# Turning x for the scores: TensorE transposes, or 32x32 squares and VectorE

## The chip, the cores and the metric

The kernel runs on one core of one Trainium2 chip. The metric is the time of one execution on the device in microseconds; lower is better. Runs are given as a median with the lowest and highest.

## What is computed

```python
def _attn_ref(x, state) -> np.ndarray:
    B, H, S, D = x.shape                     # 8, 8, 512, 64; state has Ns = 32 rows
    scale = 1.0 / np.sqrt(D)
    scores = scale * np.matmul(x, state.transpose(0, 1, 3, 2))
    ...
    xread = np.matmul(a, state)              # a: softmax of scores over the state rows
    scores2 = scale * np.matmul(state, x.transpose(0, 1, 3, 2))
    ...
    sread = np.matmul(a2, x)                 # a2: softmax of scores2 over the 512 tokens
    return np.concatenate([xread, sread], axis=2).astype(np.float32)

def _moe_ref(x, w_in, w_out) -> np.ndarray:  # 4352 tokens x 512, d_ff 2048
    h = x @ w_in
    g = h * (1.0 / (1.0 + np.exp(-1.702 * h)))
    return (g @ w_out).astype(np.float32)
```

Each batch of x meets its state in both directions, and the two results, side by side for all heads, go through an MLP. All of it is float32. `scores2` contracts over D, so TensorE needs x with D on the partitions (x turned); `sread` contracts over tokens and needs x as it lies in memory.

## The kernel before

The work goes batch by batch, b = 0 to 7. While the second matrix of the MLP is applied to batch b, the attention and the first matrix are prepared for batch b + 1. Batches 0 and 1 and the weights, which arrive as float64 words and are rounded on the chip, take the first part of the span, up to about 155 us. From b = 2 on the iterations are alike.

Products are made by Strassen's scheme of seven products, and inside some of these again (`strassen_low`). The seven outer products for a batch are called P1 to P7, and are run in the order P1, P2, P5, P6, P3, P7, P4. P1, P2 have two halves, "a" and "b". P5, P6, P3, P7 and P4 are, from b = 2 on, each seven small products of eight matmuls; after the i-th of these comes the slot "P5.i" and so on. Each small product ends in a PSUM bank, and VectorE adds it to an earlier one (L656), or ScalarE copies it (L660, L666). Three banks are used in turn, x, y and z: y takes products 2, 5 and 7, z takes 4 and 6, and a later product accumulates on what the earlier one left, so it waits until the add before it has read the bank.

The order of instructions on every engine is the order in which the program issues them; nothing is reordered. Waits between engines follow from the tiles that are read and written. `hooks_next(b)` is a table of the work for the next batch: the name of a slot, and the step that is issued there. `strassen_two` runs through the products and calls `hook(name)` at each slot. So the table decides what stands behind what in each engine's queue.

The steps that matter here, for batch b, in slots of the iteration b - 1:

- `load_x(b)`: four transfers of 256 KB, 128 tokens each, into the tile `xn` (one buffer, 16 KB a partition). They are issued from SyncE (SP) after the last product of the iteration b - 2. In between, the same buffer holds `low4`, the sums that P4 of the running iteration needs, which are loaded after `att_sread`.
- `att_xT(b, j)`: four TensorE transposes of 128x128 (L282) of two heads, and one copy to SBUF by ScalarE (L283). It is called for j = 0 to 3, in the slots P1a and P1b.
- `att_scores(b)`: 8 matmuls of 512 columns (L303), from the turned x, in P2a. Both softmaxes start from their result.
- `att_blocks`, `x_max`, `x_sub`, `x_exp`, `x_sum`, `x_inverse`, `x_scale`, `x_back`: the softmax over the state rows, after VectorE has turned the scores in squares of 32x32 (L334). At the end it turns them back (L429). g = 0, 1 are its two halves.
- `att_s_max`, `att_s_exp`, `att_s_norm`: the softmax over tokens.
- `att_sread(b)`: 64 matmuls with x as it lies (L462).
- `up_strassen(b)`: the first matrix of the MLP at the beginning of the iteration b; its products end in adds on VectorE (L1053). The last two of these follow the first half of P1.
- `s12`, `s3` (L523, L524, L529) and the L709 adds: sums of activations for the outer and inner products. `own6` places two of these steps into P6.
- `load_weights`: the 16 pieces of each weight matrix, issued from SP as room for them comes free (L168).

In memory, x is [batch, head, token, d], with rows of 64 floats. In the turned tile, 128 partitions are two heads (g) by 64 values of d, and the free side is j (four pairs of heads) by 512 tokens.

All transfers of the kernel are issued from SP. The framework gives each of them one of eight semaphores in turn, and a transfer waits for the one eight before it to land.

Of the kernel before, what the change touches and what calls it, by code (L numbers as in the profile page):

```python
# [10 lines left out]
FP32 = mybir.dt.float32  # L11
I32 = mybir.dt.int32
U32 = mybir.dt.uint32
AF = mybir.ActivationFunctionType
# [6 lines left out]
def kernel(  # L21
# [30 lines left out]
    nc = tc.nc  # L52

    B, H, S, D = x.shape
    Ns = state.shape[2]
    DM = H * D
    DF = moe_w_in.shape[1]
    P = 128
    NPR = P // Ns
    NG = H // NPR  # L60
    NF = DF // P
# [5 lines left out]
    HF, HN = NF // 2, DM // 2  # L67
    scale = float(1.0 / np.sqrt(D))
# [3 lines left out]
    out_x = out.rearrange("(b t) n -> b t n", b=B)[:, :S].rearrange("b (c q) n -> b c q n", c=SCH)  # L72
    out_s = out.rearrange("(b t) n -> b t n", b=B)[:, S:]
    x_v = x.rearrange("b h (c q) d -> b c q h d", c=SCH)
    st_v = state.rearrange("b (j g) n d -> b g j n d", g=NG)

    konst = ctx.enter_context(tc.tile_pool(name="konst", bufs=1))
    xpool = ctx.enter_context(tc.tile_pool(name="xpool", bufs=1))
# [44 lines left out]
            nc.tensor.matmul(ps, zeros[:, :P], zeros, start=True, stop=True)  # L123


    xn, stn = {}, {}

    def load_state(b):
        stn[b] = apool.tile([P, NG, D], FP32, tag="stn", name=f"stn_{b}", bufs=2)
# [3 lines left out]
    def load_x(b):  # L133
        if b == 1:
            xn[b] = sums[:, 0].rearrange("p (c h d) -> p c h d", c=SCH, h=H)
        else:
            xn[b] = xpool.tile([P, SCH, H, D], FP32, tag="xn", name=f"xn_{b}")
        for c in range(SCH):
            nc.sync.dma_start(xn[b][:, c], x_v[b, c])

    def x_heads(b, c, j):
        return xn[b][:, c, NG * j : NG * (j + 1)].rearrange("q g d -> q (g d)")
# [33 lines left out]
    for i, v in enumerate((8.0 * most, 8.0 * (most - least))):  # L176
        t = konst.tile([P, 1], FP32, name=f"edge_{i}")
# [90 lines left out]
    A = {b: {} for b in range(B)}  # L268
# [134 lines left out]
        t = a["e1"][:, g]  # L403
        nc.vector.tensor_tensor(out=t, in0=t, in1=a["mx"][:, g].to_broadcast((P, NB, Ns)), op=ALU.subtract)

    def x_exp(b):
        nc.scalar.activation(out=A[b]["e1"], in_=A[b]["e1"], func=AF.Exp, scale=scale)

    def x_sum(b, g):
        a = A[b]  # L410
# [102 lines left out]
    def quarters(key, u, ntok):  # L513

        g, half = G[key, u], ntok // 2
        return g[:, :, :half], g[:, :, half:ntok]

    def s12(key, u, ntok):

        half = ntok // 2  # L520
        (a11, a21), (_, a22) = quarters(key, u, ntok), quarters(key, HF // 2 + u, ntok)
        s1, s2 = S1[:, 2 * u : 2 * u + 2, :half], S2[:, 2 * u : 2 * u + 2, :half]
        nc.vector.tensor_tensor(out=s1, in0=a21, in1=a22, op=ALU.add)  # L523
        nc.vector.tensor_tensor(out=s2, in0=s1, in1=a11, op=ALU.subtract)  # L524
# [156 lines left out]
    def strassen_two(key, dst, hooks, a4):  # L681
# [4 lines left out]
        g = [G[key, u] for u in range(HF)]  # L686
# [30 lines left out]
        def low_banks():  # L717
            return [bank_o[1], *(psH.tile([P, FC], FP32, tag="h", name=f"low_{key}") for _ in range(2))]
# [50 lines left out]
        o, h0, h1 = low_banks()  # L769
# [6 lines left out]
        else:  # L776
# [9 lines left out]
            o, h0, h1 = low_banks()  # L786
# [33 lines left out]
        def y_of(u0, o):  # L820
            return lambda u, i: g[u0 + u][:, :, o + P * i : o + P * (i + 1)]
# [3 lines left out]
        own6 = {}  # L825
        if not plain:
            steps12, left12 = sums(y_of(NU, 0), r)
            own6 = {5: steps12[:1], 6: steps12[1:2]}
        lowly("P6", left_of(S2, q1, q2, q4), T2, low_a, banks, k2, own6)
        if not plain:  # L830
            low_load(3, 0)
# [2 lines left out]
        if plain:  # L834
# [5 lines left out]
            o, h0, h1 = low_banks()  # L840
            lowly("P7", left3, T3, low_b, [h0, h1, o], k3, {})
        else:
            hook("P6")
            p3 = o01
            o, h0, h1 = low_banks()
# [7 lines left out]
            o, h0, h1 = low_banks()  # L853
# [11 lines left out]
        if not plain:  # L865
            o, h0, h1 = low_banks()
# [15 lines left out]
    def hooks_next(b):  # L882

        h = {}

        def at(name, fn, *args):
            h.setdefault(name, []).append((fn, args))

        at("P1a", att_state, b)
        at("P1a", att_xT, b, 0)  # L890
        at("P1b", att_xT, b, 1)
        at("P1b", att_xT, b, 2)
        at("P1b", att_xT, b, 3, True)
        at("P2a", att_scores, b)
        at("P2a", att_M, b, 0)
        at("P2a", att_M, b, 1, True)
        at("P2a", att_blocks, b)
        at("P2a", att_s_max, b)
        at("P2a", att_s_exp, b)
        for g in range(NG):  # L900
            at("P2a", x_max, b, g)
            at("P2a", x_sub, b, g)
        at("P5.1" if b > 2 else "P2a", x_exp, b)
        if b > 2:
            at("P5.6", att_s_norm, b)
        else:
            at("P2", att_s_norm, b)
        steps = up_sums(b)

        A[b]["sums"] = {0: steps[9:11], 1: [steps[11], steps[14]]}  # L910
        attention = [
            ("P6.1", x_sum, 0), ("P6.2", x_sum, 1), ("P6.3", x_inverse), ("P6.4", x_scale, 0), ("P6", att_eT, 0), ("P6", att_eT, 1),
        ]
        if b > 2:
            attention += [("P3.3", x_scale, 1), ("P3.4", x_back, 0), ("P3.5", x_back, 1)]
            names = {"T": range(5), "P7.5": (5, 6), "P7.6": (7,), "P4.1": (8,), "P4.5": (12, 13)}
            run, turned = "run", "P7.2"
        else:
            attention += [("P6.5", x_scale, 1), ("P6.6", x_back, 0), ("P6", x_back, 1)]
            names = {"P3a": range(7), "P7.1": (7,), "P7.2": (8,), "P7.3": (12, 13)}  # L920
            run, turned = "P3a", "P3b"
        attention += [(run, att_sread), (run, att_M, 3, True), (run, att_M, 2)]
        for name, fn, *args in attention:
            at(name, fn, b, *args)
        for name, n in names.items():
            for i in n:
                at(name, steps[i][0], *steps[i][1])
        at(turned, att_srT, b)
        return h
# [174 lines left out]
    def rounds(n):  # L1104
        round_to(done["b"] + n)
# [80 lines left out]
    def T_of(t, x0, x1):  # L1186
        nc.vector.tensor_tensor(out=t, in0=x0, in1=x1, op=ALU.subtract)
# [3 lines left out]
    for f in range(NF):  # L1191
        rounds(1)
        round_to(NFC * NPR + f + 1)
        for r in range(SCH):
            down(0, r, [f], out_x[0, r], r == SCH - 1)
        if f in (0, 2):
            for g in range(NG):
                att_eT(f // 2, g)
        if f in (0, nper * 2):
            att_M(1, 2 + f // (nper * 2))  # L1200
        if f in (1, 3):
            att_sread(f // 2)
        if f in (2, 4):
            att_srT(f // 2 - 1)
        if f % 2 == 1:
            up_x(1, rest.pop(0))
        if f == NF - 4:
            load_state(2)
            load_x(2)
        if f == NF - 2:  # L1210
            T_of(T1, B12, B11)
            for u in range(NU - 1):
                s12(1, u, S)
            T_of(T2, B22, T1)
        if f == NF - 1:
            for u in range(NU - 1):
                s3(1, u, S)
            T_of(B12, B22, B12)
    s12(1, NU - 1, S)
    s3(1, NU - 1, S)  # L1220

# [3 lines left out]
    for b in range(1, B):  # L1225
        if b > 1:
            ahead = {"P1a": [(up_strassen(b, S, *parts_x(b), A[b]["sums"]), ())]}
            if b == 2:
                ahead["P3.6"] = [(low_third, (T4,))]
        else:  # L1230
            ahead = {
                "P1a": low_sums(T2, low_a)
                + [(low_keep, (2, turn_rooms[0])), (T_of, (T4, B21, T2)), (low_third, (T2,))],
                "P1b": low_sums(T3, low_b) + [(low_keep, (3, turn_rooms[1])), (low_third, (T3,))],
                "P4.7": low_sums(T1, low_b) + [(low_keep, (5, turn_rooms[1])), (low_third, (T1,)), (low_third, (B22,))],
            }
            for k, step in zip((4, 5, 6), low_sums(B22, low_a)):
                ahead[f"P7.{k}"] = [step]
            ahead["P7.6"] += [(low_keep, (6, turn_rooms[0])), (low_load, (2, 0))]
        if b + 1 < B:  # L1240
            hooks = hooks_next(b + 1)
        else:

            steps, left, right = sr_sums()
            order = (
                ("P5.6", 2), ("P6.1", 3), ("P6.2", 6), ("P6.3", 7), ("P6.4", 8), ("P3.3", 9), ("P3.4", 10), ("P3.5", 11),
                ("P7.5", 12), ("P7.6", 13), ("P4.1", 16, 17), ("P4.5", 18, 19), ("P4.6", 14), ("P4.7", 15),
            )
            hooks = {name: [steps[i] for i in n] for name, *n in order}
            hooks["P3.6"] = [(low_third, (T1,))]  # L1250
            hooks["P4.7"] += [(low_third, (t,)) for t in (T2, T3, T4, B22)]
            ahead["P1a"][:0] = [steps[i] for i in (0, 1, 4, 5)]
        for name, first in ahead.items():
            hooks[name] = first + hooks.get(name, [])
        a4 = {}

        at = hooks.setdefault("run" if b > 1 else "P3a", [])
        k = 3 if b + 1 < B else 0
        at[k:k] = [(low4_load if b > 1 else low4_make, (a4,))]
        strassen_two(b, out_of(b), hooks, a4 if b > 1 else None)  # L1260
        if b + 2 < B:
            load_state(b + 2)
            load_x(b + 2)
    nb = P // Ns
    strassen(
        "sr", B * Ns, lambda r, n: out_s[nb * r.start : nb * r.stop, :, n],
# [32 lines left out]
```

## Time and profile before

| what | value |
|---|---|
| time, 3 runs | 729.72 us median (729.7 to 729.77) |
| profiled run: time, span of the core | 729.73 us, 727.9 us |
| granted TensorE clock | 0.999 |
| TensorE busy (PE), its weight loads (PEld) | 714.2 us (98%), 571.0 us (78%) |
| VectorE (DVE), ScalarE (ACT) busy | 574.6 us (79%), 252.5 us (35%) |
| transfers | 62.13 MB, mean 85 GB/s |
| TensorE transposes of x, batches 2 to 7 | 96, 273 ns each in the record, pipelined |

The span is the profiler's, of one execution; the times are those of whole executions on the device. Busy time of PE is of pipelined matmuls, whose ends overlap. In the timeline, a row is a start in us, a duration, an engine with the line of the program, the operation with its tiles, and in brackets the idle time of the engine before it with what ended it. A chain is followed back from the last instruction to what released each; its rows are a start, a duration and what ran. SPq is the queue of SyncE, which issues transfers.

### The profile page before, as it was taken

The numbers are of one execution on the slowest core, as the hardware profiler recorded it, in microseconds if no ns is written. First come the engines' busy times: TensorE is split into PE (matmuls) and PEld (weight loads), VectorE is DVE, ScalarE is ACT, GpSimd is POOL, SyncE is SP. The second block draws the span as 40 slices with busy tenths as digits, with TensorE's granted clock in tenths as the row PEclk, the third lists the DMA queues.
The fourth block names the chain that finished last, engine by engine and source line by source line (L and its number), as shares of the span: only waits on it lengthen the run. The fifth ranks groups of instructions, "written<-read, shape, count | busy, mean of one in ns | idle before, by whom it ended". The sixth has DMA issues, their size and how long they took to land.

```text
span 727.9 us, 12341 instructions
## 1 busy us (share of the span) xinstructions
PE 714.2 (98%) x5047; PEld 571.0 (78%) x5047; DVE 574.6 (79%) x1175; ACT 252.5 (35%) x486; POOL 0.8 (0%) x8
## 2 busy tenths in 40 slices
PE   8989999999999999999999999999999999999996
PEld 3433444467898798889998899889987998899995
DVE  6998899729877988788877897698788887889440
ACT  4686411024224422434234423451343324200210
POOL 0000000000000000000000000000000000000000
PEclk9999999999999999999999999999999999999999
DMA  9921245012161034302440145003420340022001
GB/s 232 353 88 58 88 145 148 0 59 102 45 205 30 1 102 162 74 1 65 162 112 1 34 156 149 1 15 99 170 56 1 102 146 30 1 93 82 15 1 29
DMA packets 53672, 62.13 MB, mean 85 GB/s; under 512 B 36976, under 2 KB 44656, under 8 KB 53616
## 3 DMA queue, kind: packets, MB, share of 16 engines
q1 hardware_dynamic: 53616, 61.35, 26.8%
q8 instruction: 39, 0.64, 0.3%
q14 instruction: 17, 0.14, 0.1%
HBM read 48.50 MB, written 12.85 MB: 84 GB/s over the span
## 4 chain that ended last, share of the span: by engine, by line
PE 92%; DVE 3%; ACT 2%; DMA 2%; issue 0%; SPq 0%; DVEq 0%; ACTq 0%
PE low L651 17%; PE o L1043 16%; PE o L702 16%; PE o L651 8%; PE o L500 8%; PE h L482 7%; PE upx L1043 6%; PE M L303 4%; PE o L543 2%; PE xT L282 2%; PE o L303 1%; PE sr L462 1%; PE warm L123 1%; DMA out_dram<-osb_sr 1%; PE eT L451 1%; DMA xn<-in_x_dram 1%
## 5 line engine op out<-in xcount | busy, mean ns | idle before, releaser
L1053 DVE TENSOR_TENSOR g<-o,g 128x512 f32<-128x512 f32 (+1 forms) x140 | 88.0, 650 | 67.5 <-PE o L1043 66.6
L702 PE MATMUL o<-w_out,g 128*128 128x256 f32 x480 | 108.9, 381 | 0.0
L702 PEld LDWEIGHTS o<-w_out,g 128*128 128x128 f32 x480 | 89.6, 190 | 17.7 <-issue 6.3
L1050 ACT ACTIVATE g<-g 128x512 f32<-128x512 f32 (+1 forms) x84 | 49.8, 600 | 101.8 <-DVE g L1053 101.8
L1043 PE MATMUL upx<-aT,M 128*128 128x256 f32 x192 | 49.3, 379 | 0.0
L1043 PE MATMUL o<-ta,M 128*128 128x256 f32 x192 | 49.3, 379 | 0.0
L1043 PE MATMUL o<-ta,ms 128*128 128x256 f32 x192 | 48.3, 379 | 0.0
L442 ACT COPY M<-M 128x512 f32<-128x512 f32 x64 | 33.2, 597 | 37.7 <-PE M L303 37.7
L1043 PEld LDWEIGHTS o<-ta,ms 128*128 128x128 f32 x192 | 36.5, 190 | 5.0
L1043 PEld LDWEIGHTS o<-ta,M 128*128 128x128 f32 x192 | 36.5, 190 | 5.0
L651 PE MATMUL low<-low,g 128*128 128x128 f32 x304 | 40.2, 275 | 0.0
L1043 PEld LDWEIGHTS upx<-aT,M 128*128 128x128 f32 x192 | 36.1, 190 | 4.7
L651 PEld LDWEIGHTS low<-low,g 128*128 128x128 f32 x304 | 37.0, 192 | 0.0
L651 PE MATMUL low<-sums,later 128*128 128x128 f32 x264 | 34.9, 275 | 0.0
L523 DVE TENSOR_TENSOR later<-g,g 128x512 f32<-128x512 f32 (+1 forms) x32 | 20.8, 649 | 17.6 <-ACT g L485 17.6
L651 PEld LDWEIGHTS low<-sums,later 128*128 128x128 f32 x264 | 32.7, 192 | 0.4
L303 PE MATMUL M<-w_in,stT 64*32 64x512 f32 x512 | 32.7, 594 | 0.2 <-ACT eT L452 0.2
L482 PE MATMUL h<-low,M 128*128 128x512 f32 x64 | 29.8, 600 | 1.4 <-DVE low L391 1.4
L482 PE MATMUL h<-aT,M 128*128 128x512 f32 x64 | 28.7, 599 | 1.4 <-ACT M L442 1.4
L500 PE MATMUL o<-w_out,g 128*128 128x512 f32 x64 | 28.7, 594 | 0.0
L651 PE MATMUL low<-w_out,g 128*128 128x128 f32 x216 | 28.5, 275 | 0.0
L500 PE MATMUL o<-w_out,sums 128*128 128x512 f32 x64 | 28.4, 594 | 0.0
(213 smaller groups left out, 1307.5 us busy)
## 6 DMA issues: line engine op xcount, KB each, us to landing
low<-low SPq DMA_DIRECT2D x34, 768.0 KB
later<-in_moe_w_out_dram SPq DMA_DIRECT2D x16, 512.0 KB
xn<-in_x_dram SPq DMA_DIRECT2D x28, 256.0 KB
w_out<-in_moe_w_in_dram SPq DMA_DIRECT2D x12, 512.0 KB
out_dram<-osb SPq DMA_DIRECT2D x18, 256.0 KB
out_dram<-later SPq DMA_DIRECT2D x14, 256.0 KB
later<-in_moe_w_in_dram SPq DMA_DIRECT2D x4, 512.0 KB
sums<-in_x_dram SPq DMA_DIRECT2D x4, 256.0 KB
```

The source lines that it names most:

```text
L282: nc.tensor.transpose(ps[:, c], x_heads(b, c, j), ident)
L303: nc.tensor.matmul(ps[g][st], A[b]["stT"][rows, st], rhs(rows, j), start=True, stop=True)
L442: nc.scalar.copy(m[:, g], ps[g])
L482: nc.tensor.matmul(hps, lhs[i], rhs[i], start=(i == 0), stop=(i == n - 1))
L500: nc.tensor.matmul(ops, G[key, f // 2][:, f % 2, P * r : P * (r + 1)], w_out[:, f], start=(f == 0), stop=(f == NF - 1))
L523: nc.vector.tensor_tensor(out=s1, in0=a21, in1=a22, op=ALU.add)
L543: nc.tensor.matmul(ps[:, r], lhs[f][:, P * r : P * (r + 1)], rhs[:, f], start=(first and r == 0 and f == 0), stop=(f == HF - 1), skip_grou ...
L651: nc.tensor.matmul(ps, lhs[f], rhs[:, f], start=(first and f == 0), stop=(f == QF - 1), skip_group_check=True)
L702: nc.tensor.matmul(ps[:, r], lhs[f][:, P * r : P * (r + 1)], rhs[:, f], start=(r == 0 and f == 0), stop=(f == HF - 1), skip_group_check=True,)
L1043: nc.tensor.matmul(ps[:, k], lhs[i][:, o : o + P], rhs[i], start=(first and k == 0 and i == 0), stop=(i == n - 1), skip_group_check=True,)
L1050: nc.scalar.activation(out=dst, in_=src, func=AF.Gelu_apprx_sigmoid)
L1053: nc.vector.tensor_tensor(out=dst, in0=ps, in1=x, op=ALU.add)
```

## The change

x of batches 2 to 7 is now loaded twice. The first load, `load_x_squares`, is made of 16 transfers a batch. Each fills 32 partitions, which are 32 tokens of each group of 32, with pieces of 32 values of d (128 bytes), for one pair of heads, one g and one half of d; so the tile `xsq` holds squares of 32 tokens by 32 values at the place where the turned square belongs. `turn_x` has VectorE turn each square in place, in four instructions of 128x512, and the tile is then what `att_xT` made. `att_xT` is no longer called for these batches. The second load, `load_x`, is issued after `att_scores` into the same room, for `att_sread`.

`turn_x(b + 1)` stands between the main part of `up_strassen(b)` and `strassen_two(b)`, for b = 2 to 6; on VectorE it comes right ahead of the last two L1053 adds. For batch 2 it stands ahead of the last sums of batch 1, and its squares are issued when f is 8 and not 12, which puts them ahead of the last piece of `w_out` in SP's queue.

Further, for batches above 2, the second half of `x_max`, `x_sub` and `x_exp` is moved from P2a and P5.1 to P5.6, P5.7 and P6.1. `x_sum` of the second half is moved from P6.2 to P6.3 for all of them. The two `own6` steps are moved from P6.5 and P6.6 to P6.2 and P6.5.

```diff
+    x_sq = x.rearrange("b (j g) (t q) (k a) -> b g k q j t a", g=NG, q=Ns, a=Ns)
...
+    def load_x_squares(b):
+        xsq[b] = xpool.tile([P, NPR, S], FP32, tag="xn", name=f"xsq_{b}")
+        for g in range(NG):
+            for k in range(D // Ns):
+                o = D * g + Ns * k
+                dst = xsq[b][o : o + Ns].rearrange("p j (t a) -> p j t a", a=Ns)
+                for j in range(NPR):
+                    nc.sync.dma_start(dst[:, j], x_sq[b, g, k][:, j])
+
+    def turn_x(b):
+
+        A[b]["xT"] = xsq[b]
+        for j in range(NPR):
+            nc.vector.transpose(xsq[b][:, j], xsq[b][:, j])
...
-    def x_exp(b):
-        nc.scalar.activation(out=A[b]["e1"], in_=A[b]["e1"], func=AF.Exp, scale=scale)
+    def x_exp(b, g=slice(None)):
+        t = A[b]["e1"][:, g]
+        nc.scalar.activation(out=t, in_=t, func=AF.Exp, scale=scale)
...
-            own6 = {5: steps12[:1], 6: steps12[1:2]}
+            own6 = {2: steps12[:1], 5: steps12[1:2]}
...
         at("P1a", att_state, b)
-        at("P1a", att_xT, b, 0)
-        at("P1b", att_xT, b, 1)
-        at("P1b", att_xT, b, 2)
-        at("P1b", att_xT, b, 3, True)
         at("P2a", att_scores, b)
+
+        at("P2a", load_x, b)
...
-        for g in range(NG):
-            at("P2a", x_max, b, g)
-            at("P2a", x_sub, b, g)
-        at("P5.1" if b > 2 else "P2a", x_exp, b)
+        at("P2a", x_max, b, 0)
+        at("P2a", x_sub, b, 0)
         if b > 2:
+            at("P5.1", x_exp, b, 0)
             at("P5.6", att_s_norm, b)
+            at("P5.6", x_max, b, 1)
+            at("P5.7", x_sub, b, 1)
+            at("P6.1", x_exp, b, 1)
         else:
+            at("P2a", x_max, b, 1)
+            at("P2a", x_sub, b, 1)
+            at("P2a", x_exp, b)
             at("P2", att_s_norm, b)
...
-            ("P6.1", x_sum, 0), ("P6.2", x_sum, 1), ("P6.3", x_inverse), ("P6.4", x_scale, 0), ("P6", att_eT, 0), ("P6", att_eT, 1),
+            ("P6.1", x_sum, 0), ("P6.3", x_sum, 1), ("P6.3", x_inverse), ("P6.4", x_scale, 0), ("P6", att_eT, 0), ("P6", att_eT, 1),
...
-        if f == NF - 4:
+        if f == HF:
             load_state(2)
-            load_x(2)
+            load_x_squares(2)
...
             T_of(B12, B22, B12)
+            turn_x(2)
...
+            if b > 1:
+                turn_x(b + 1)
             hooks = hooks_next(b + 1)
...
             load_state(b + 2)
-            load_x(b + 2)
+            load_x_squares(b + 2)
```

More of the change, by code (lines that the diff above doesn't have):

```diff
@@ L123, in keep_warm @@
             nc.tensor.matmul(ps, zeros[:, :P], zeros, start=True, stop=True)
-    xn, stn = {}, {}
+    xn, xsq, stn = {}, {}, {}
     def load_state(b):
```

## The prediction

> **What bounds the kernel now.** I read the chain that ended last first, then the busy shares, then one batch of the steady part in time order, then the queues beside it. The page's chain:
>
> ```profile
> PE 92%; DVE 3%; ACT 2%; DMA 2%; issue 0%; SPq 0%; DVEq 0%; ACTq 0%
> ```
>
> TensorE is the chain. In the windows of the steady iterations, 78.1 us each, it is busy for the whole of each at a granted clock of 1.00. So a TensorE instruction taken out is worth its full pitch, as long as nothing else then ends last. The chain in order of time, where the work on x of the next batch sits:
>
> ```profile
> 389.58 3.45 PE o L702 x16
> 393.04 1.73 PE o L1043 x8
> 394.76 0.11 PE stT L272
> 394.87 0.44 PE xT L282 x4
> 395.31 3.46 PE o L702 x16
> 398.76 1.31 PE xT L282 x12
> 400.08 3.46 PE o L702 x16
> ```
>
> The 16 transposes take 0.44 + 1.31 = 1.75 us of chain a batch, 109 ns each, with no wait around them. The next thing to see is what VectorE does meanwhile, from its timeline:
>
> ```profile
> 389.62 1.42 DVE L1053 TENSOR_TENSOR g<-o,g 128x512 f32<-128x512 f32 x2 [0.24 <-PE o L1043]
> 393.94 0.69 DVE L1053 TENSOR_TENSOR g<-o,g 128x512 f32<-128x512 f32 x1 [2.90 <-PE o L1043]
> ...
> 408.78 0.68 DVE L399 TENSOR_REDUCE mx<-e 128x16 f32<-128x512 f32 x1
> ...
> 411.81 0.29 DVE L656 TENSOR_TENSOR pu<-low,pu 128x128 f32<-128x128 f32 x1 [0.43 <-PE low L651]
> ...
> 418.06 0.29 DVE L656 TENSOR_TENSOR pu<-o,pu 128x128 f32<-128x128 f32 x1 [0.97 <-PE o L651]
> ...
> 419.78 0.29 DVE L656 TENSOR_TENSOR later<-low,pu 128x128 f32<-128x128 f32 x1 [0.23 <-PE low L651]
> ```
>
> The brackets are its idle time and who ended it: 2.90 us before 393.94, then nothing worth a bracket until 411.81. In P5 and P6 (from 409.75 and 416.00) it adds up each product of 0.89 us in 0.29 us, with other work between; it is less than a microsecond ahead of TensorE there. And the transfers of x, from the queue's timeline and the windows:
>
> ```profile
> 369.97 3.00 SPq L139 DMA_DIRECT2D xn<-in_x_dram  x4
> ```
>
> ```profile
> 371.00:372.00 1.00, 1.00 (x7) 0.87 (x6) 0.51 (x1) 0.22 (x1) 0.00 (x0) 1.00 0.89 204
> 372.00:373.00 1.00, 1.00 (x6) 0.89 (x5) 0.97 (x3) 0.06 (x1) 0.00 (x0) 1.00 1.29 275
> 375.00:376.00 1.00, 1.00 (x6) 0.90 (x5) 1.00 (x2) 0.54 (x1) 0.00 (x0) 1.00 0.96 155
> 376.00:377.00 1.00, 1.00 (x6) 0.87 (x6) 0.03 (x1) 1.00 (x3) 0.00 (x0) 1.00 0.01 3
> ```
>
> The last two columns are DMA share and GB/s: 1 MB in 4096 pieces of 256 B is through by 376, 6 us after its first issue.
>
> **What the Trainium skill says.** "VectorE: DVE Perf Modes", The three transpose paths: VectorE turns 32x32 blocks only, about as fast as TensorE turns a whole tile (311 against 390 ns for 128x128 bf16). The trace has larger fp32 tiles on VectorE, 702 ns each, and TensorE's pitch of 109 ns for a 128x128 tile:
>
> ```profile
> L429 DVE STREAM_TRANSPOSE aT<-e 128x512 f32<-128x512 f32 x12 | 8.4, 702 | 0.0
> ```
>
> "DMA: Bandwidth & Descriptors", Why small descriptors are slow (HBM only): a packet from HBM costs its 32 B beats and about 3 cycles more, 11 for 256 B, so 7 for 128 B. How a descriptor splits into AXI transactions, there: a read that starts off a 256 B boundary fetches from the boundary. Half of the squares start 128 B off, so an estimate is 7 to 11, never much more than a 256 B piece. No run here shows 128 B pieces yet. "SBUF — State Buffer", SBUF: two separate sides: transfers and engines use separate ports, so the load itself shouldn't slow the engines; TensorE at 1.00 through 371 to 376 agrees.
>
> **The change part by part.**
>
> TensorE loses 16 transposes in each of six batches: 6 x 1.75 = 10.5 us of chain. Nothing takes their place on its queue. ScalarE loses four copies of 593 ns, off the chain.
>
> VectorE gets four transposes of 128x512 before the last L1053 pair of the up products, that is in the 2.90 us gap at 391.04 to 393.94. From the 702 ns row, and a spacing of some 0.65 us where two follow each other (a pair at L334 takes 1.30), four take 2.65 to 2.8 us. They fit, with 0.1 to 0.3 us to spare; the gap is 2.90 us in each of the five iterations b = 2 to 6. I take nothing; in place is not shown by any row, so a second pass would cost up to 2.8 us more, and nothing excludes a few tenths. For batch 2 the transposes go into the 14.05 us in which VectorE waits before 160.12: nothing.
>
> The squares: 16 transfers of 64 KB in 512 pieces of 128 B, 8192 pieces a batch. They start where x was loaded, at 369.97; VectorE wants them at 391.04, 21 us later. 4096 pieces took some 4.9 us on 16 engines, 19 ns a piece and engine; at the same cost 512 pieces an engine take 9.8 us, at 7/11 of it 6.2 us. The issue is 0.75 us for a transfer of 1024 pieces, 0.58 us for a small one of state: 16 of them 9 to 12 us. As built, each waits for the eighth before it to land; 8 issues are 4.6 to 6 us, above the 2.2 us that a store takes to land (the osb waits), so this hardly adds. The last lands at 369.97 + 12 + 2 = 384 at worst: 7 us early. The same queue has nothing else to issue until 409, so what it is moved past is free. For batch 2 the squares go ahead of the sixteenth piece of w_out: it is issued about 10 us later than at 115.3, lands by 128, and VectorE wants it at 126.5. A delay of 2 us ends in VectorE's idle 3.52 us before 138.44: nothing, bounded by 3 us of idle.
>
> x as it is: four transfers behind the scores (its room is the squares'), issued at 403, landed by 409 as above; att_sread wants it at 429.5. SP waits for the scores, and behind it stands the store of osb, ready at 409.4. Hidden by 20 us.
>
> The edits of order. Half of x_max, x_sub and x_exp move from P2a to P5.6, P5.7 and P6.1, for batches above 2. TensorE now reaches P5 at 408.00; VectorE's list up to x_sub of the first half is unchanged and ends where x_max of the second began, 408.78. Then osb (0.6), one s4 (0.68): ready for the first P5 add at 410.06. That add can start at 411.81 - 1.75 = 410.06. So 1.75 us taken from TensorE, 1.32 from VectorE, and the slack of 0.43 is gone: no stall yet. Through P5 each add stays just in time as before. At P5.6 and P5.7 x_max and x_sub come in: the c21 add at 414.97 (ready 414.46), x_sub to 415.87, x_sum to 416.5, the first P6 add 416.50 (ready 416.31). Then the step brought forward from P6.5 (0.67), x_sum of the second half, the inverse (0.56): the c22 add at 418.65 to 418.94, ready at 418.03. TensorE's sixth product of P6 accumulates on that bank and was due at 420.47 - 1.75 = 418.72. It waits 0.28 us. After that P6.6 is free of its old step and VectorE is just in time again. So an iteration gives 1.75 - 0.28 = 1.47 us; I bound the stall by 0 and 1 us, since each tenth by which VectorE is late at 393.94 is added to it one to one.
>
> Iteration b = 1 (batch 2 ahead) keeps its order. There VectorE runs without idle from 160.12, where ScalarE's copies of osb release it, to 183.8, whatever TensorE does. TensorE comes to P6 at 178.71 and not 180.46, and its fifth and sixth products need the adds that end at 182.64 and, no longer waiting, 184.14: stalls of about 0.46 and 0.60 us. It gives 0.69 us, bounds 0.3 and 1.75. In b = 7 the step moved to P6.2 makes the c22 add 0.4 us late, on a slack of about 0.6: 0.1 us lost.
>
> Sum: 5 x 1.47 + 0.69 - 0.1 = 7.9 us. Against the profiled span of 727.9 us that is 720.0. The profiled run's time is 729.73, 1.8 above its span and at the median of the runs shown, so 721.8 us.
>
> **The rivals.**
>
> All of it. If the adds have more room than I read, the whole 10.5 us is kept: 719.2 us. For it: no TensorE wait shows anywhere in the steady part. Against: the brackets of 0.43, 0.97 and 0.23 us are all the room that VectorE has, and TensorE comes 1.75 us sooner.
>
> VectorE becomes the bound. If in-place transposes take 0.95 us, the four overrun the gap by 0.9 us; with no idle until P5 that comes out as stall, 0.9 x 5 = 4.5 us less gain: 726.3 us.
>
> Squares land late, the slower side. VectorE stands at the first transpose with the L1053 pair, all s12 and s3 sums and the P5 sums behind it. Lateness passes through to TensorE, and it costs more than it saves from a landing at about 392.7. That takes 22 us for 512 pieces an engine, 43 ns a piece. At twice the 22 ns of engine time that a 256 B piece shows (5.7 us of share x 16 / 4096) the load takes 512 x 44 ns = 22.5 us from the first data at 371.2, to 393.7, some 2.5 us late past the slack: (2.5 - 1.47) x 5 - 0.6 = 4.6 us slower, 734.3 us. Against: half the bytes a piece, and 7 us in hand.
>
> The change not doing what it says: the transposes might be covered anyway. The chain, with no wait on either side, excludes it.
>
> **How the numbers follow.** My case 0.70; all of it 0.12; VectorE the bound 0.12; late squares 0.06. The likeliest gives 721.8. The range runs from the full gain, 719.0, to 725.0, which takes in a stall of 0.9 us in each iteration; left out are the worse part of the third case and the fourth. This kernel's measurement can tell about 0.2%, 1.5 us, from no change: faster 0.91 (the first two and nearly all of the third), within it 0.03, slower 0.06.
>
> **What would show it.** No TensorE transposes at L282 but batch 1's; the in-place transposes at 0.65 to 0.70 us in a gap, ended by no DMA; the iteration at 76.7 us and not 78.1; in P6 a TensorE wait of 0.2 to 0.4 us on a VectorE add, none in P1 to P5; the squares through within 14 us. A transpose that waits for the load of x, or an iteration above 78 us, makes it wrong.

## The result and the profile after

| | before | after |
|---|---|---|
| time, 4 runs each | 729.75 us (729.7 to 729.79) | 720.42 us (720.36 to 720.46) |
| ratio, with 95% interval | | 0.9872 [0.9855, 0.9889] |
| span of the profiled run | 727.9 us | 718.7 us |
| one steady iteration | 78.14 us | 76.43 us |
| DVE, ACT busy | 574.6, 252.5 us | 586.4, 241.6 us |
| transfers | 62.13 MB, 53672 packets | 68.43 MB, 104361 packets |

The kernel became 9.3 us faster; 7.9 was forecast. The iterations are measured from the start of one `up_strassen` chain to the next, which is at 210.87, 289.00 and 367.13 us before and at 209.99, 286.42 and 362.85 us after. Lines of the program have moved: the up products are L1064 and their adds L1074 (L1043, L1053 before), the outer products L720 (L702), the small products L669 (L651), their adds L674 (L656), other sums L727 (L709), the scores L320 (L303). The turn is L156, the load of the squares L150. The stretch shown before now lies some 4.3 us earlier.

The page's chain, after:

```profile
PE 88%; DVE 5%; DMA 3%; ACT 2%; SPq 1%; issue 1%; DVEq 0%; ACTq 0%
```

TensorE is still the chain. The shares of DVE and DMA have grown because the chain is now led through VectorE in batch 1's stretch, of which more below. There the page also leads it through the second load of x (5.98 us from 171.25), but VectorE's rows show no wait for that load, and the run without it ("No turn", below) is no faster. The chain in order of time, after (start, duration, what ran):

```profile
385.30 3.45 PE o L720 x16
388.75 1.73 PE o L1064 x8
390.48 0.11 PE stT L289
390.59 6.91 PE o L720 x32
397.50 1.02 PE o L320 x16
...
414.60 0.94 PE low L669 x8
```

Where 0.44 and 1.31 us of transposes stood between two outer products, 32 matmuls now follow one another for 6.91 us. The last row is the sixth small product of P6: its step in the chain is 0.94 us and not 0.89, the only stall of the iteration. It accumulates on the bank that the add at 414.10 (below) reads; the prediction calls this the c22 add. VectorE's timeline of the same stretch, after:

```profile
386.67 2.48 DVE L156 STREAM_TRANSPOSE xsq<-xsq 128x512 f32<-128x512 f32 x4
389.65 0.69 DVE L1074 TENSOR_TENSOR g<-o,g 128x512 f32<-128x512 f32 x1 [0.50 <-PE o L1064]
...
391.12 0.68 DVE L541 TENSOR_TENSOR later<-g,g 128x512 f32<-128x512 f32 x1
...
405.78 0.29 DVE L674 TENSOR_TENSOR pu<-low,pu 128x128 f32<-128x128 f32 x1
...
414.10 0.23 DVE L674 TENSOR_TENSOR later<-low,pu 128x128 f32<-128x128 f32 x1
```

The turn has no bracket, so it waited for no transfer. It takes 2.48 us in the idle 2.90, and 0.50 us of that gap is left, since the next instruction can start a little before the last turn is through. The idle 0.43, 0.97 and 0.23 us in front of the adds of P5 and P6 are gone: VectorE runs from the last up add to the add of P6's last product (416.47, 0.48 us idle) without an idle time worth a bracket, and TensorE still waits for nothing but the 0.05 us. SP's timeline, and two windows (the last two columns are the DMA share and GB/s), after:

```profile
365.69 9.38 SPq L150 DMA_DIRECT2D xsq<-in_x_dram  x16
398.80 2.78 SPq L141 DMA_DIRECT2D xn<-in_x_dram  x4
```

```profile
375.00:376.00 1.00, 1.00 (x6) 0.90 (x5) 1.00 (x3) 0.81 (x2) 0.00 (x0) 1.00 0.76 126
376.00:377.00 1.00, 1.00 (x7) 0.87 (x6) 1.00 (x2) 0.00 (x0) 0.00 (x0) 1.00 0.19 30
```

The squares are through at about 376.2, 10.5 us after the first issue and 10 us before VectorE asks for them at 386.67. The buffer that they, x as it lies and the sums of P4 share in turn is 8 KB a partition (1 MB in all), and not 16 KB as the description of the kernel has it.

Batch 1's iteration has stalls of another kind. TensorE's timeline there, after:

```profile
182.44 1.16 PE L669 MATMUL low<-sums,later 128*128 128x128 f32 x8
183.78 1.16 PE L669 MATMUL o<-sums,g 128*128 128x128 f32 x8 [0.18 <-DVE later L674]
```

These are the fifth and sixth products of P6. By the pitch of 0.89 us they were due at 182.13 and 183.33; they wait for VectorE's adds by 0.31 and 0.45 us, and the seventh follows another 0.10 late.

The sum, measured: batch 2 starts 0.88 us sooner, the next five iterations are together 8.47 us shorter (four of them by 1.70 or 1.71, the fifth by 1.67), and the last gives back 0.1 us: 0.88 + 8.47 - 0.1 = 9.2 us, the difference of the spans.

### The profile page after: what moved, and what is told of

Same layout as the page of the kernel before. It is cut to its first block, busy times and chain, and to the rows that moved or that the text cites. A ratio compares the mean times of both kernels' runs of the same rounds, so it can differ in the third digit from the quotient of the medians.

```text
span 718.7 us, 12329 instructions
## 1 busy us (share of the span) xinstructions
PE 704.6 (98%) x4949; PEld 561.7 (78%) x4951; DVE 586.4 (82%) x1199; ACT 241.6 (34%) x467; POOL 0.8 (0%) x8
## 2 busy tenths in 40 slices
DMA packets 104361, 68.43 MB, mean 95 GB/s; under 512 B 87664, under 2 KB 95344, under 8 KB 104304
## 4 chain that ended last, share of the span: by engine, by line
PE 88%; DVE 5%; DMA 3%; ACT 2%; SPq 1%; issue 1%; DVEq 0%; ACTq 0%
PE low L669 17%; PE o L1064 17%; PE o L720 14%; PE o L669 8%; PE o L518 7%; PE h L500 7%; PE upx L1064 6%; PE M L320 4%; PE o L561 2%; DMA xn<-in_x_dram 2%; PE o L320 1%; PE sr L480 1%; PE warm L125 1%; DMA out_dram<-osb_sr 1%; PE eT L469 1%; DMA out_dram<-osb 1%
## 5 line engine op out<-in xcount | busy, mean ns | idle before, releaser
L1074 DVE TENSOR_TENSOR g<-o,g 128x512 f32<-128x512 f32 (+1 forms) x140 | 88.0, 650 | 55.5 <-PE o L1064 54.6
L720 PE MATMUL o<-w_out,g 128*128 128x256 f32 x480 | 107.9, 381 | 0.0
L720 PEld LDWEIGHTS o<-w_out,g 128*128 128x128 f32 x480 | 90.2, 190 | 18.3 <-issue 6.3
L1064 PE MATMUL upx<-aT,M 128*128 128x256 f32 x192 | 49.3, 379 | 0.0
L1064 PE MATMUL o<-ta,M 128*128 128x256 f32 x192 | 49.3, 379 | 0.0
L1064 PE MATMUL o<-ta,ms 128*128 128x256 f32 x192 | 48.3, 379 | 0.0
L1064 PEld LDWEIGHTS o<-ta,ms 128*128 128x128 f32 x192 | 36.5, 190 | 4.9
L1064 PEld LDWEIGHTS o<-ta,M 128*128 128x128 f32 x192 | 36.5, 190 | 4.9
L669 PE MATMUL low<-low,g 128*128 128x128 f32 x304 | 40.2, 275 | 0.0
L1064 PEld LDWEIGHTS upx<-aT,M 128*128 128x128 f32 x192 | 36.1, 190 | 4.7
L669 PEld LDWEIGHTS low<-low,g 128*128 128x128 f32 x304 | 37.0, 192 | 0.0
L669 PE MATMUL low<-sums,later 128*128 128x128 f32 x264 | 35.0, 276 | 0.1
L669 PEld LDWEIGHTS low<-sums,later 128*128 128x128 f32 x264 | 32.7, 192 | 0.7 <-DVE pu L674 0.3
L320 PE MATMUL M<-w_in,stT 64*32 64x512 f32 x512 | 32.6, 594 | 0.2 <-ACT eT L470 0.2
L669 PE MATMUL low<-w_out,g 128*128 128x128 f32 x216 | 28.5, 275 | 0.0
```

Of the source, the lines that this page charges most:

```text
L320: nc.tensor.matmul(ps[g][st], A[b]["stT"][rows, st], rhs(rows, j), start=True, stop=True)
L669: nc.tensor.matmul(ps, lhs[f], rhs[:, f], start=(first and f == 0), stop=(f == QF - 1), skip_group_check=True)
L720: nc.tensor.matmul(ps[:, r], lhs[f][:, P * r : P * (r + 1)], rhs[:, f], start=(r == 0 and f == 0), stop=(f == HF - 1), skip_group_check=True,)
L1064: nc.tensor.matmul(ps[:, k], lhs[i][:, o : o + P], rhs[i], start=(first and k == 0 and i == 0), stop=(i == n - 1), skip_group_check=True,)
L1074: nc.vector.tensor_tensor(out=dst, in0=ps, in1=x, op=ALU.add)
```

## The experiments

### The edits of order alone, on the kernel before

```diff
-            own6 = {5: steps12[:1], 6: steps12[1:2]}
+            own6 = {2: steps12[:1], 5: steps12[1:2]}
...
+            at("P5.6", x_max, b, 1)
+            at("P5.7", x_sub, b, 1)
+            at("P6.1", x_exp, b, 1)
...
-            ("P6.1", x_sum, 0), ("P6.2", x_sum, 1)
+            ("P6.1", x_sum, 0), ("P6.3", x_sum, 1)
```

> The kernel before with the order edits alone, and x still turned by TensorE. Theory: TensorE is the chain without a wait and VectorE has slack, so moving VectorE's work gives nothing: 729.8 us, within 0.5 us of the kernel before. Rival (the edits of order bring part of the gain by themselves): 728 us or less.

Measured: 730.11 us (730.0 to 730.35), ratio 1.0006 [0.9997, 1.0014]. Alone the new order of VectorE's list gains nothing, since TensorE waited for nothing in P5 and P6; it is 0.4 us slower, and no run of it is as fast as the slowest of the 15 of the kernel before that were taken beside it. The 0.1 us that the changed kernel gives back in its last iteration is there in this run too.

### The change without its edits of order

The diff is the one above the other way round, on the changed kernel.

> The squares and the turning stay; x_max, x_sub, x_exp, x_sum and the two own6 steps go back to the slots they had before. Theory (VectorE's list is what limits how much of the 1.75 us an iteration keeps): VectorE has 1.32 us more ahead of the first P5 add, which in the changed kernel is ready just in time, so the sixth product of P5 waits about 0.5 us in each of five iterations: 722.6 us, the iteration at about 76.9 us instead of 76.43. Rival (VectorE has room, the order edits do nothing): 720.4 us and 76.4 us.

Measured: 724.27 us (724.2 to 724.48), ratio 0.9925 [0.9909, 0.9942]; the iteration is 77.18 us. The order is worth 3.85 us once the transposes are gone, 1.7 more than the time I had expected here leaves for it. The timeline of all engines in P5, of this kernel:

```profile
407.40 0.68 DVE L727 TENSOR_TENSOR osb<-o,g 128x512 f32<-128x512 f32 x1
...
408.13 1.16 PE L669 MATMUL o<-low,spare_M 128*128 128x128 f32 x8
...
410.12 0.28 DVE L674 TENSOR_TENSOR spare_M<-o,pu 128x128 f32<-128x128 f32 x1
...
410.46 1.16 PE L669 MATMUL o<-sums,spare_M 128*128 128x128 f32 x8 [0.27 <-DVE spare_M L674]
```

With the second x_max and x_sub still ahead of it, the osb sum (first row, the sum that goes out of the kernel) comes at 407.40 us. It reads the bank that the fourth product of P5 fills: that starts at 408.13, due at 407.97. I had overlooked this one. Then the fifth starts 0.11 late, and the sixth, due at 410.02, waits 0.44 for the add at 410.12, which its bracket names. These three make 0.71 of the 0.79 us (1.75 less 0.96) that an iteration loses to waits; the seventh product follows 0.10 late. The moves were tried only together. The waits shown come from x_max and x_sub ahead of P5; whether the moves of x_sum and of the own6 steps are needed too, the runs do not show.

### No turn: x loaded as it is, and given to the scores unturned

x of batches 2 to 7 is loaded once only, as it lies in memory: no squares, no second load, no VectorE transposes of x.

```diff
         A[b]["xT"] = xsq[b]
-        for j in range(NPR):
-            nc.vector.transpose(xsq[b][:, j], xsq[b][:, j])
+        A[b]["xT"] = xn[b].rearrange("p c h d -> p (c h d)").rearrange("p (j t) -> p j t", j=NPR)
...
-        at("P2a", load_x, b)
...
-            load_x_squares(b + 2)
+            load_x(b + 2)
```

> The changed kernel without squares, without turning and without the second load: x of batches 2 to 7 is loaded once as it lies, and the scores are taken from it unturned, so the scores and all that follows from them are of other data. Theory (the turning is hidden whole in VectorE's gap, the squares behind the up products, the second load behind P5): the time stays that of the changed kernel, 720.4 us within 0.5 us. Rival (squares, turning or the second load cost something on the path): 719 us or less.

Measured: 720.59 us (720.5 to 720.69), ratio 0.9875 [0.986, 0.9889]. That is the changed kernel's time, and 0.2 us more. So everything that the change adds (2.48 us of VectorE, 16 small-piece transfers and a second megabyte a batch) costs nothing that can be measured.

### Two needless turns more

```diff
             nc.vector.transpose(xsq[b][:, j], xsq[b][:, j])
+        for _ in range(2 if b > 2 else 0):
+            nc.vector.transpose(xsq[b][:, 0], xsq[b][:, 0])
```

> The changed kernel with the first quarter of the squares turned twice more, in batches 3 to 7 (three turns are one). Two transposes at 0.62 us are 1.24 us more in a gap with 0.50 us left, so VectorE is 0.74 us late at the last up adds. Theory (no idle on VectorE from there to P5, and the adds of P5 and P6 just in time): TensorE stalls by about 0.7 us in each of five iterations, 723.9 us. Rival (the adds have room of their own): 720.4 to 721 us.

Measured: 720.45 us (720.38 to 720.49), ratio 0.9873 [0.9858, 0.9887]: not a tenth of a microsecond lost, and my expectation missed. VectorE's timeline, of this kernel:

```profile
389.08 1.42 DVE L158 STREAM_TRANSPOSE xsq<-xsq 128x512 f32<-128x512 f32 x2
390.42 1.25 DVE L1076 TENSOR_TENSOR g<-o,g 128x512 f32<-128x512 f32 x2
391.59 0.67 DVE L543 TENSOR_TENSOR later<-g,g 128x512 f32<-128x512 f32 x1
...
406.16 0.28 DVE L676 TENSOR_TENSOR pu<-low,pu 128x128 f32<-128x128 f32 x1
...
409.29 0.29 DVE L676 TENSOR_TENSOR spare_M<-o,pu 128x128 f32<-128x128 f32 x1
```

Against the rows of the changed kernel, VectorE is 0.77 us late at the first of the two up adds (390.42 for 389.65) and 0.47 after them (391.59 for 391.12), because the second add no longer waits for its product. It is 0.38 late at the first add of P5 (406.16 for 405.78), 0.19 at the next (407.68 for 407.49), and 0.01 at the fourth (409.29 for 409.28). TensorE starts P5 at the same time, 403.73 for 403.72. This much lateness isn't passed on: TensorE asks for an add only two or three products after the one it reads, and in between VectorE makes up 0.1 to 0.2 us a product, in waits that are too short for a bracket in the changed kernel's rows.

### Four needless turns more

The same with 4 for 2, to find where that room ends.

> As with two more turns, but four more of the first quarter, batches 3 to 7. Two left VectorE 0.47 us late at the last up adds, and TensorE did not wait, since a product of P5 gives VectorE 0.89 us for some 0.80 us of work and TensorE needs the first add only before its fifth product, 1.2 us after it is due. Two more dependent turns add 1.34 us: 1.8 us late. Theory (the room is about 1.2 us at the first add and 0.1 us a product, and what goes beyond stalls TensorE): 0.6 us at the fifth product and some 0.6 us at the fourth or sixth, about 1.2 us an iteration, 726 us. Rival (VectorE's lateness does not matter here at all): 720.5 us.

Measured: 727.68 us (727.49 to 727.74), ratio 0.9969 [0.9957, 0.9981]. The iteration is 77.86 us, 1.43 longer than the changed kernel's. The timeline of all engines in P5, of this kernel:

```profile
407.33 0.69 ACT L372 ACTIVATE e<-o,mx 128x512 f32<-128x512 f32 x1 [1.63 <-DVE mx L361]
...
408.80 0.26 ACT L680 COPY pu<-low 128x128 f32<-128x128 f32 x1
409.11 1.16 PE L671 MATMUL low<-sums,later 128*128 128x128 f32 x8 [0.56 <-ACT pu L680]
...
412.39 1.16 PE L671 MATMUL o<-sums,spare_M 128*128 128x128 f32 x8 [0.28 <-DVE spare_M L676]
```

VectorE's late maximum holds ScalarE's two exponentials, and behind them on ScalarE stands the copy of P5's first product, which the third product needs: 0.73 us late (409.11, due 408.38). The next two lose 0.10 and 0.07, and the sixth 0.44 on VectorE's add: 1.34 of the 1.43 us; the seventh follows 0.10 late. So the price is real, but it begins later than I had put it: 0.47 us of lateness after the up adds cost nothing, 1.96 us cost 1.43 (this L543 row is at 395.96, 4.84 us after the changed kernel's, of which 2.88 are the later start of its iteration). And part of it comes through ScalarE.

### The squares in 32 and in 64 transfers a batch

```diff
-                    nc.sync.dma_start(dst[:, j], x_sq[b, g, k][:, j])
+                    for i in range(0, NB, NB // 2):
+                        v = slice(i, i + NB // 2)
+                        nc.sync.dma_start(dst[:, j, v], x_sq[b, g, k][:, j, v])
```

> Each transfer of squares cut into two, 32 a batch, the same pieces and bytes. At 0.40 to 0.59 us an issue they take 13 to 19 us; the last lands 14 to 21 us after the first issue, and VectorE asks for it at 21.0. Theory (the load is hidden as long as it lands within 21 us): 720.4 us, at most 1 us more. Rival (the squares are already on the edge of the path): several us slower.

Measured: 720.58 us (720.42 to 720.96), ratio 0.9875 [0.9861, 0.989]. The issue takes 16.97 us and not 9.38, and the squares are through at about 383.5, 3 us before VectorE turns them at 386.54. The time stays: there was room.

> Each transfer of squares cut into four, 64 a batch, the same pieces and bytes. At 0.40 to 0.59 us an issue they take 26 to 38 us, 6 to 17 us too late for VectorE. Theory (lateness past the gap's 0.5 us goes to TensorE one to one, with VectorE standing at the first transpose that waits for the load): 5 x (5.5 to 16.5) us more, 748 to 803 us, about 776. Rival (the wait of VectorE is covered by the products of P1 and P2): under 730 us.

Measured, with 4 for 2: 774.88 us (773.51 to 776.13), ratio 1.0618 [1.0602, 1.0634], 54.5 us above the changed kernel: 7.6 of them are lost before batch 2 starts (its squares are cut as well), and 8.4 to 12.0 in each of the five iterations. SP's timeline and VectorE's, of the kernel with 64:

```profile
394.02 31.62 SPq L152 DMA_DIRECT2D xsq<-in_x_dram  x64
```

```profile
413.66 1.42 DVE L1076 TENSOR_TENSOR g<-o,g 128x512 f32<-128x512 f32 x2 [0.25 <-PE o L1066]
421.37 0.71 DVE L158 STREAM_TRANSPOSE xsq<-xsq 128x512 f32<-128x512 f32 x1 [6.29 <-DMA xsq<-in_x_dram]
```

This is the rival of squares that land late, made true. VectorE stands for 6.29 us at the first turn and for 1.23, 1.05 and 1.17 at the other three, which each wait for their own transfers. After the up adds it is 9.33 us late (its L543 row is at 428.77), and this iteration is 8.79 us longer than the changed kernel's. The lateness after the up adds, measured from the start of each iteration, and what it costs, of the runs with more turns and of this one:

| run | VectorE late after the up adds | iteration longer by | difference |
|---|---|---|---|
| two more turns | 0.47 us | 0 | |
| four more turns | 1.96 us | 1.43 us | 0.53 us |
| 64 transfers, iteration shown | 9.33 us | 8.79 us | 0.54 us |
| 64 transfers, the one with the latest squares | 12.50 us | 11.97 us | 0.53 us |

So there is a room of 0.53 us, and past it lateness goes to TensorE in full. While TensorE stands here, its granted clock falls too (0.50 from 428 to 434 us). That adds nothing to the time: TensorE has to wait for VectorE's side again at 441.91, for 1.22 us, and the difference in the table is the same as with four more turns. The run without the edits of order fits the same room: 1.32 us of work ahead of P5, less 0.53, is the 0.79 us that it loses to waits.

### Batch 1's stall: one up product sooner

The last up product of batch 1 goes ahead of the last outputs of batch 0, so that VectorE can begin its run of sums sooner.

```diff
+        if f == NF - 1:
+            up_x(1, rest.pop(0))
         for r in range(SCH):
             down(0, r, [f], out_x[0, r], r == SCH - 1)
...
-        if f % 2 == 1:
+        if f % 2 == 1 and f < NF - 1:
             up_x(1, rest.pop(0))
```

> The changed kernel with the last up product of batch 1 issued before the last step of the second matrix of batch 0, not after it, so its gelu stands ahead of the four output copies on ScalarE. Theory (in the iteration of batch 1 TensorE loses 1 us to VectorE's adds, because VectorE's list starts only at 160 us, when ScalarE is through with copies that wait for each other's store): VectorE starts some 8 us earlier, the 1 us comes back: 719.5 us. Rival (VectorE's list is bound by something else there): 720.4 us.

Measured: 719.65 us (719.56 to 719.7), ratio 0.9862 [0.9846, 0.9878]. VectorE's timeline at the start of its run of sums, of the changed kernel and of this one, and TensorE's sixth product of P6 in this one:

```profile
160.03 0.69 DVE L541 TENSOR_TENSOR later<-g,g 128x512 f32<-128x512 f32 x1 [11.54 <-ACT g L503]
```

```profile
152.10 0.69 DVE L541 TENSOR_TENSOR later<-g,g 128x512 f32<-128x512 f32 x1 [3.70 <-ACT g L503]
```

```profile
182.94 1.06 PE L669 MATMUL o<-sums,g 128*128 128x128 f32 x8
```

VectorE begins 7.93 us sooner, and the products of P6 follow at their pitch of 0.89 us without a wait. It is the fastest version here, 0.77 us below the changed kernel, with no run in common. Batch 2 starts at 209.05 us, 0.94 sooner than in the changed kernel and 1.82 sooner than before: batch 1's iteration now keeps its whole 1.75.

The same edit on the kernel before:

> The kernel before, with the last up product of batch 1 issued ahead of the last step of the second matrix of batch 0. Theory (that VectorE's list starts at 160 us costs TensorE something only once TensorE's transposes are gone): no change, 729.7 us within 0.3 us. Rival (the late start cost the kernel before as well): 728.9 us.

Measured: 731.36 us (730.08 to 731.93), ratio 1.002 [1.0013, 1.0027]: slower by 1.6 us where I expected nothing. The timelines of TensorE and ScalarE, of this kernel:

```profile
163.27 1.58 PE L282 MATMUL xT<-ident,xn 128*128 128x128 f32 x12 [0.84 <-ACT stT L274]
```

```profile
162.47 0.58 ACT L507 COPY osb<-o 128x512 f32<-128x512 f32 x1 [3.94 <-DMA out_dram<-osb]
```

The outputs of batch 0 come 1.72 us later by the moved product, and so do the first three of ScalarE's four copies of them, within 0.03 us. The fourth comes 3.47 us later, at 162.47, since it waited 3.94 us for a store to leave its buffer, where the two copies before it waited 2.17. The stT and xT copies stand behind it, and TensorE's transposes wait for them. With a wait of 2.2 us the fourth copy would have started at 160.7 and that of stT ended at 161.5, before TensorE is ready for the transposes at 162.3; this is an estimate from these rows. So by this estimate the moved product alone costs nothing here, and what costs is the slow store. In the packet records of this run, 120 of the store's 128 packets are through by 160.21, and the last eight start at 160.88, when a packet of 16 KB of an instruction queue (159.60 to 160.89) has ended. That this packet held them back was not tried, and whether the other runs of this kernel, 730.08 to 731.93 us, all have the slow store is not known.

Batch 2 starts at 212.02 and not 210.87, and the iterations are as long as before. The rest of the profiled run's 1.5 us falls at the very end, where 0.40 us ahead of VectorE's last outputs (osb_sr) have no cause that the profile shows, and 0.04 in the kernel before. The changed kernel has no transposes that wait for such copies in that place, so there the edit is a gain.

## Why the prediction was right, and where its terms were off

**The chain.** TensorE's transposes were worth their full pitch: 1.75 us taken out, 1.71 us kept. The run without turns has the same time, so nothing added stands against it.

**The gap.** Four turns were to take 2.65 to 2.8 us in a gap of 2.90. They took 2.48, in place, 0.60 us from one to the next, with 0.50 us to spare. No second pass, no wait for a transfer. "VectorE: DVE Perf Modes", The three transpose paths, holds here in what matters: VectorE turns squares of 32x32 only. The change rests on that, with the transfer placing each square and VectorE turning it where it lies, at 676 ns for 128x512.

**The squares.** At worst they were to land 14 us after the first issue; they took 10.5. The issue set this, as the prediction had it, and not the pieces. The DMA share from 366 to 377 us sums to 6.75 us, and 6.75 x 16 / 8192 is 13 ns of engine time a piece, against the 22 ns of a 256 B piece. This is 0.6 of it, close to the 7 to 11 of "DMA: Bandwidth & Descriptors", Why small descriptors are slow. The 22 ns come from a stretch with a share above 1, where times of pieces overlap, so the agreement is a rough one. The starts off a 256 B boundary cost nothing visible: in the packet records the mean time of a piece is 12.0 to 12.3 ns in fifteen of the sixteen transfers, those with such starts among them.

**The second load.** It was to be hidden by 20 us and is: issued at 398.80, used at 423.49, and its absence changes nothing.

**P5 and P6.** No stall in P5, one in P6 at the c22 add for the sixth product: the mechanism and the place were right, the size was not. The stall is 0.05 us and not 0.28. I had the c22 add 10.65 us after the start of P5; it came after 10.38 (414.10 less 403.72) and takes 0.23 us and not 0.29. I had counted the second maximum, its subtraction and the reciprocal ahead of it some 0.1 us too long each. The instruction behind each of them doesn't need its result, and starts 0.58, 0.60 and 0.27 us after it, sooner than the 0.67, 0.68 and 0.35 us that these last. Five times 0.23 us is 1.15 of the 1.4 us by which the forecast was short, and batch 1 is 0.19.

**Batch 1.** The stalls were to be 0.46 and 0.60 us, and are 0.31 and 0.45; 0.88 us was kept where 0.69 was forecast. The cause, VectorE's unbroken run from the outputs of batch 0 on, is shown by the run with one up product sooner, which keeps the whole.

**What was wrong without consequence.** That each tenth of a us by which VectorE is late at 393.94 is added to the stall one to one failed: 0.77 us of lateness there cost nothing. The second add takes up 0.30 of it and the room behind takes 0.53, so the first 0.8 us are free, and what goes beyond does count one to one. The rival in which VectorE becomes the bound at an overrun of 0.9 us was therefore priced far too high: about 0.1 us an iteration, by this estimate, and not 0.9. The turns were not slow, so this did not bear on the result. The rival in which all is kept, 719.2 us, was nearer to the result than its chance of 0.12 said.

**The edits of order.** The prediction counted them as part of the path and never as a gain by themselves. The runs confirm it: 3.85 of the 9.3 us need them, and they are worth nothing alone.

## What to carry to other kernels

Where one engine is the chain, an instruction taken from it is worth its full pitch only if the other engines' lists have room behind it: bring the replacement into a measured idle gap, and move as much work from ahead of the next deadline as the gain takes away. Room isn't the idle time in the brackets alone: count for each add which later product needs it, and whether the engine catches up before then. Here the brackets of that stretch were gone, and 0.53 us of room were left. Take copies on a third engine into the count too, since they stand behind whatever is late in its queue.

## What the runs showed of the hardware

An in-place VectorE turn of 128x512 float32 runs as fast as one into another tile, 676 ns in the mean against 702 ns at L429, and 0.60 us from one to the next. Where each turns the same part again, on the other's result, they take 0.67 to 0.71 us each (two from 389.08 to the next instruction at 390.42 in the run with two more turns, four from 391.95 to 394.79 in the run with four).

The load of the squares is paced by the number of its transfers and not by its pieces. 16 transfers of 512 pieces take 0.59 us each on SP, 32 of 256 take 0.53, 64 of 128 take 0.49, so half the pieces in a transfer hardly shorten it. The DMA share is 0.75, then 0.41, then 0.22, where x in 256 B pieces reached 1.34: the 16 engines stand idle for part of the time. Most issues take 0.49, 0.45 and 0.43 us in the three runs. One in each of the loads of this stretch takes 1.4 to 1.7 us, and a packet of 16 KB of an instruction queue runs at the same time (369.99 to 370.95 us in the changed kernel); that it is the cause was not tried. It is the ninth, the tenth and the eighth issue, so it is not the wait for the transfer eight before, of which these issues show no other sign.
